# GroupNorm on one core: all stores issued from ScalarE's queue, and the last store in one piece

## Chip, core and metric

The kernel runs on one core of a Trainium2 chip. The metric is the device time of one execution in microseconds. A core has TensorE (PE), VectorE (DVE), ScalarE (ACT), GpSimd (POOL) and SyncE (SP). SP and ACT can issue transfers, which 16 DMA engines carry out.

## What is computed

A group normalisation of x, 128 x 1024 x 32 x 16 in bf16, with 32 groups of 32 channels:

```python
def reference(x, g, b):
    G = 32
    ...
    xr = x.reshape(B, G, C // G, H, W)
    mu = xr.mean(axis=(2, 3, 4), keepdims=True)
    var = ((xr - mu) ** 2).mean(axis=(2, 3, 4), keepdims=True)
    xn = (xr - mu) / jnp.sqrt(var + 1e-5)
    xn = xn.reshape(B, C, H, W)
    return xn * g[None, :, None, None] + b[None, :, None, None]
```

134 MB are read and 134 MB written.

## The kernel before

Two samples make a tile of 128 partitions x 8192 elements (2 MB): a partition holds 16 channels of one sample, and a pair of partitions is a group. There are 64 tiles, i = 0 to 63, in 11 buffers (`XBUFS`), normalised in place. Each tile goes through these steps, each a function of the code:

- L(i), line 121: SP issues the load.
- M1(i), line 137: ACT sums the last 2048 of the 8192 elements (from tile 2 on). M(i), line 154: PE sums the other 12 pieces of 512 over the partition pair, into PSUM.
- R(i), line 171: DVE reduces that to the negative mean.
- Q(i), line 189: ACT squares the tile less its mean and adds up, 7.12 us. Gm(i), line 206: PE sums over the pair.
- T(i), line 221: ACT takes the square root of the variance.
- A(i), lines 232 to 255: DVE makes the reciprocal, scale and bias, and normalises in 16 instructions.
- S(i), lines 264 to 274: SP issues the store. The last store, i = 63, is two transfers: partitions 0 to 119, then 120 to 127.

The loop runs these as a pipeline, s from -1 to 65. In iteration s the order in which instructions are recorded is M1(s+1), M(s+1), Gm(s-1), A(s-2), R(s+1), Q(s), T(s-1), S(s-2), L(s+7). Nine loads go out ahead of the loop (`PREFETCH`). `chain` fixes the order of each engine's instructions as they are recorded; so ACT's list repeats M1(s+1), Q(s), T(s-1), and SP's repeats S(s-2), L(s+7).

Waits are put in by the framework. Three kinds matter here. A load waits until the store that used its buffer has landed. An engine waits for data that another one makes: T(s-1) is recorded with a wait for R(s+1), which follows A(s-2) on DVE. And the transfers of both queues count their completions on eight semaphores, DMAHW0 to DMAHW7, handed out in rotation in the order of the program; a transfer is issued only when the previous one on its semaphore has landed, unless another wait implies that.

Of the kernel before, what the change touches and what calls it, by code (L numbers as in the profile page):

```python
# [24 lines left out]
def kernel(  # L25
# [7 lines left out]
    nc = tc.nc  # L33
    P = nc.NUM_PARTITIONS
# [5 lines left out]
    NT = B0 // NS  # L40
# [16 lines left out]
    o_v = out.rearrange("(t n) (cb k) h w -> t (n cb) (k h w)", n=NS, cb=CB)  # L57
# [19 lines left out]
    def chain(key, inst):  # L77
        prev = last.get(key)
        if prev is not None:
            tc.add_manual_dep(inst.ins, prev.ins.name, nosync, reason="pipeline order")  # L80
        last[key] = inst
        return inst
# [5 lines left out]
        out=ind_f[:].rearrange("p (a c) -> p a c", c=PPG),  # L88
        in_=ones_f[:].rearrange("p (a c) -> p a c", c=PPG),
# [7 lines left out]
        out=ind_f[:].rearrange("p (a c) -> p a c", c=PPG),  # L97
        in_=ind_f[:].rearrange("p (a c) -> p a c", c=PPG),
# [165 lines left out]

    def S(i):
        st = state[i]
        xt = st["xt"]
        if i == NT - 1:
            lo = P - P // 16
            chain("sp", nc.sync.dma_start(out=o_v[i][0:lo, :], in_=xt[0:lo, :]))  # L270
            chain("sp", nc.sync.dma_start(out=o_v[i][lo:P, :], in_=xt[lo:P, :]))
        else:
            chain("sp", nc.sync.dma_start(out=o_v[i], in_=xt[:]))
        state.pop(i - 3, None)

    for i in range(min(PREFETCH, NT)):
# [16 lines left out]
    for s in range(-1, NT + 2):  # L293
        if 0 <= s + 1 < NT:
            M1(s + 1)
            M(s + 1)
        if 0 <= s - 1 < NT:
            Gm(s - 1)
        if 0 <= s - 2 < NT:
            A(s - 2)  # L300
        if 0 <= s + 1 < NT:
            R(s + 1)
        if 0 <= s < NT:
            Q(s)
        if 0 <= s - 1 < NT:
            T(s - 1)
        if 0 <= s - 2 < NT:
            S(s - 2)
            if s - 2 + PREFETCH < NT:
                L(s - 2 + PREFETCH)  # L310
# [30 lines left out]
```

## Time and profile before

| | |
|---|---|
| median of 3 runs | 642.97 us (642.89 to 643.67) |
| the profiled execution's own time | 642.89 us |
| its span in the profile | 641.1 us |
| loads issued from SP | 64 of 2048 KB, 24.2 us to landing |
| stores issued from SP | 63 of 2048 KB, 28.7 us to landing; then 1920 KB and 128 KB |
| moved | 268.69 MB, mean 419 GB/s |
| Q on ACT, line 189 | x64, 7122 ns each |
| M1 on ACT, line 137 | x62, 1898 ns each |
| normalising on DVE, line 255 | x1024, 406 ns each |
| last store issued | 620.41 and 620.88 us from the span's start |

Busy time is summed over an engine's instructions and given as a share of the span. A "q" behind an engine's name is its sequencer, which reads the instructions, does the waits and issues transfers; those are not counted as busy. The time to landing runs from the issue to the last of a transfer's completions.

### The profile page before, as it was taken

Reading aid. Unit: us, or ns where it says so; the run is one execution under the profiler, and the core shown is the slowest. Engines: PE = TensorE matmul, PEld = TensorE weight load, DVE = VectorE, ACT = ScalarE, POOL = GpSimd, SP = SyncE. Lnnn points to the kernel's source line nnn. Section 1 sums busy time; section 2 is a strip of 40 time slices with the busy share of each in tenths; the row PEclk is TensorE's granted clock in tenths of the full one; section 3 lists DMA queues with packets and bytes.
Section 4 is the critical chain, followed back from the end, with each engine's and each line's share of the span. In section 5 each row is a group of like instructions: output and inputs, shape, how many; then the busy total and the mean of one; then the engine's idle time right before and its main releaser. Section 6 shows DMA issues by size and latency. Waiting matters only on the chain.

```text
span 641.1 us, 3917 instructions
## 1 busy us (share of the span) xinstructions
PE 333.1 (52%) x904; PEld 127.4 (20%) x904; DVE 420.7 (66%) x1349; ACT 590.6 (92%) x318; POOL 1.6 (0%) x6
## 2 busy tenths in 40 slices
PE   4655574556456545654664465466465454564200
PEld 1222121122112212221221122122121121222100
DVE  0076677668667766776686677667766866776760
ACT  0999999999999999999999999999999999999900
POOL 1000000000000000000000000000000000000000
PEclk9777767776776676667666766766666766767655
DMA  9999999999999999999999999999999999999993
GB/s 359 425 427 423 422 432 424 428 431 428 430 433 429 432 430 427 435 429 428 432 430 434 430 426 432 431 430 432 429 430 432 429 432 432 428 431 430 431 408 96
DMA packets 18781, 268.69 MB, mean 419 GB/s; under 512 B 2375, under 2 KB 2375, under 8 KB 2375
## 3 DMA queue, kind: packets, MB, share of 16 engines
q1 hardware_dynamic: 18759, 268.45, 98.6%
q8 instruction: 7, 0.11, 0.1%
q14 instruction: 15, 0.12, 0.0%
HBM read 134.23 MB, written 134.22 MB: 419 GB/s over the span
## 4 chain that ended last, share of the span: by engine, by line
ACT 56%; DMA 19%; issue 19%; DVE 2%; PE 1%; SPq 0%; DVEq 0%; ACTq 0%
ACT ja L189 41%; ACT ja L137 15%; DMA out_dram<-xt 14%; DMA xt<-in_x_dram 5%; DVE xt L255 2%; ACT rstd L221 1%; PE ps L154 1%; SPq L121 0%; DVE jd L171 0%; DVE scl L237 0%; DVE bia L243 0%; DVE rstd L232 0%; DVEq L336 0%; ACTq L137 0%
## 5 line engine op out<-in xcount | busy, mean ns | idle before, releaser
L189 ACT ACTIVATE ja<-xt,negmean 128x8192 bf16<-128x8192 bf16 x64 | 455.8, 7122 | 15.8 <-DVE jd L171 13.8
L154 PE MATMUL ps<-xt,ind_b 128*128 128x512 bf16 x776 | 307.7, 580 | 66.1 <-DMA xt<-in_x_dram 66.1
L255 DVE TENSOR_SCALAR xt<-xt,scl,bia 128x512 bf16<-128x512 bf16 x1024 | 336.3, 406 | 2.6 <-DVE bia L243 0.2
L154 PEld LDWEIGHTS <-ind_b 128*128 128x128 bf16 x776 | 109.1, 147 | 234.5 <-issue 164.3
L232 DVE RECIPROCAL rstd<-rstd 128x1 f32<-128x1 f32 x64 | 10.5, 163 | 168.7 <-ACT rstd L221 168.7
L137 ACT ACTIVATE ja<-xt 128x2048 bf16<-128x2048 bf16 x62 | 117.7, 1898 | 1.5 <-DMA xt<-in_x_dram 1.5
L243 DVE SCALAR_TENSOR_TENSOR bia<-scl,negmean,bet 128x16 f32<-128x16 f32 x64 | 15.0, 235 | 2.3
L237 DVE TENSOR_SCALAR scl<-gam,rstd 128x16 f32<-128x16 f32 x64 | 15.0, 234 | 2.2
L189 ACT ACTIVATION_READ_ACCUMULATOR ja<-xt,negmean 128x1 f32 x64 | 11.9, 186 | 0.0
L137 ACT ACTIVATION_READ_ACCUMULATOR ja<-xt 128x1 f32 x62 | 11.7, 189 | 0.0
L171 DVE TENSOR_SCALAR_CACHE_REDUCE jd<-ps 128x512 bf16<-128x512 f32 x2 | 1.4, 692 | 8.3 <-PE ps L154 8.3
L171 DVE TENSOR_SCALAR_CACHE_REDUCE jd<-ps,ps_170 128x512 bf16<-128x512 f32 x1 | 0.8, 756 | 6.6 <-PE ps_170 L206 6.6
L290 DVE CAST gam<-gam_b 128x16 f32<-128x16 bf16 x1 | 0.2, 175 | 6.6 <-DMA gam_b<-in_g_dram 6.6
L206 PE MATMUL ps_3186<-carry,ind_f 128*128 128x1 f32 x2 | 0.6, 364 | 6.7 <-ACT ja L189 6.7
L206 PE MATMUL ps_3157<-carry,ind_f 128*128 128x1 f32 x2 | 0.6, 363 | 4.9 <-ACT ja L189 4.9
L206 PE MATMUL ps_1959<-carry,ind_f 128*128 128x2 f32 x2 | 0.6, 365 | 4.8 <-ACT ja L137 4.8
L206 PE MATMUL ps_734<-carry,ind_f 128*128 128x2 f32 x2 | 0.6, 364 | 4.8 <-ACT ja L137 4.8
L206 PE MATMUL ps_1616<-carry,ind_f 128*128 128x2 f32 x2 | 0.6, 364 | 4.7 <-ACT ja L137 4.7
L206 PE MATMUL ps_391<-carry,ind_f 128*128 128x2 f32 x2 | 0.6, 364 | 4.7 <-ACT ja L137 4.7
L206 PE MATMUL ps_1273<-carry,ind_f 128*128 128x2 f32 x2 | 0.6, 364 | 4.6 <-ACT ja L137 4.6
L206 PE MATMUL ps_2155<-carry,ind_f 128*128 128x2 f32 x2 | 0.6, 365 | 4.6 <-ACT ja L137 4.6
L206 PE MATMUL ps_930<-carry,ind_f 128*128 128x2 f32 x2 | 0.6, 365 | 4.6 <-ACT ja L137 4.6
(319 smaller groups left out, 127.3 us busy)
## 6 DMA issues: line engine op xcount, KB each, us to landing
xt<-in_x_dram SPq DMA_DIRECT2D x64, 2048.0 KB, 24.2
out_dram<-xt SPq DMA_DIRECT2D x63, 2048.0 KB, 28.7
out_dram<-xt SPq DMA_DIRECT2D x1, 1920.0 KB, 18.9
out_dram<-xt SPq DMA_DIRECT2D x1, 128.0 KB
gam_b<-in_g_dram SPq DMA_DIRECT2D x2, 2.0 KB, 7.2
bet_b<-in_b_dram SPq DMA_DIRECT2D x2, 2.0 KB, 7.3
```

Source lines behind the costliest of these rows:

```text
L137: nc.scalar.activation(out=ja[:, 0 : na * MMN], in_=xt[:, (NMM - na) * MMN :], func=ACT.Identity, scale=-inv_n, accum_out=carry[:, 1:2],),
L154: nc.tensor.matmul(out=ps[:], lhsT=ind_b[:], rhs=xt[:, k * MMN : (k + 1) * MMN], start=(k == 0), stop=(k == npe - 1),),
L171: nc.vector.tensor_scalar(out=jd[:], in0=st["ps"][:], scalar1=-inv_n, scalar2=seed, op0=ALU.mult, op1=ALU.add, accum_out=negmean[:],),
L189: nc.scalar.activation(out=ja[:], in_=st["xt"][:], func=ACT.Square, bias=st["negmean"][:], scale=1.0, accum_out=carry[:, 0:1],),
L206: nc.tensor.matmul(out=ps2[:, 0:ncol], lhsT=ind_f[:], rhs=st["carry"][:, 0:ncol], start=True, stop=True,),
L221: nc.scalar.activation(out=rstd[:], in_=st["ps2"][:, 0:1], func=ACT.Sqrt, bias=eps_t[:], scale=inv_n),
L232: chain("dve", nc.vector.reciprocal(out=rstd[:], in_=rstd[:]))
L237: nc.vector.tensor_scalar(out=scl[:], in0=gam[:], scalar1=rstd[:], scalar2=None, op0=ALU.mult),
L243: nc.vector.scalar_tensor_tensor(out=bia[:], in0=scl[:], scalar=negmean[:], in1=bet[:], op0=ALU.mult, op1=ALU.add,),
L255: nc.vector.tensor_scalar(out=xt[:, k * HW : (k + 1) * HW], in0=xt[:, k * HW : (k + 1) * HW], scalar1=scl[:, k : k + 1], scalar2=bia[:, k ...
L290: nc.vector.tensor_copy(out=gam[:], in_=gam_b[:])
```

## The change

`S(i)` issues the store from ACT's queue and chains it into ACT's list, so that list repeats M1(s+1), Q(s), T(s-1), S(s-2). The last store is one transfer of 128 partitions, as the others are. SP's list holds only the loads and the four small ones of gamma and beta. Nothing else is edited; the semaphores of the transfers are handed out anew.

```diff
     def S(i):
         st = state[i]
-        xt = st["xt"]
-        if i == NT - 1:
-            lo = P - P // 16
-            chain("sp", nc.sync.dma_start(out=o_v[i][0:lo, :], in_=xt[0:lo, :]))
-            chain("sp", nc.sync.dma_start(out=o_v[i][lo:P, :], in_=xt[lo:P, :]))
-        else:
-            chain("sp", nc.sync.dma_start(out=o_v[i], in_=xt[:]))
+        chain("act", nc.scalar.dma_start(out=o_v[i], in_=st["xt"][:]))
         state.pop(i - 3, None)
```

The rows of the changed program that the prediction speaks of, with what each transfer waits for in place of the semaphore's number (the store's wait for A(i) is implied by T(i+1)):

```
ACT S7  (DMAHW5) waits S3 landed
ACT S8  (DMAHW7) waits S4 landed
...
ACT S53 (DMAHW1) waits S49 landed
ACT S54 (DMAHW2) waits L60 landed
ACT S55 (DMAHW3) waits S50 landed
ACT S56 (DMAHW4) waits L61 landed
ACT S57 (DMAHW5) waits S51 landed
ACT S58 (DMAHW6) waits L62 landed
ACT S59 (DMAHW7) waits S52 landed
SP  L60 (DMAHW2) waits L56 and S49 landed
```

## The prediction

> **What bounds the kernel now.** I read the page's busy shares first, then the stretches of the span, then the order of time around the end. S(i), L(i), M1(i), Q(i), T(i), A(i) and R(i) are the code's steps for tile i, counted from 0 to 63.
>
> ```profile
> PE 333.1 (52%) x904; PEld 127.4 (20%) x904; DVE 420.7 (66%) x1349; ACT 590.6 (92%) x318; POOL 1.6 (0%) x6
> ...
> DMA  9999999999999999999999999999999999999993
> ```
>
> Two things are full: ACT (92%) and the 16 DMA engines (9 in every slice but the last).
>
> ```profile
> 100.00:600.00 500.00, 276.58 (x743) 105.24 (x741) 352.14 (x1127) 496.82 (x266) 0.00 (x0) 0.68 1.01 430
> 600.00:620.00 20.00, 1.18 (x4) 1.01 (x4) 17.19 (x57) 8.72 (x7) 0.00 (x0) 0.50 1.00 429
> ...
> 624.00:630.00 6.00, 0.00 (x0) 0.00 (x0) 0.00 (x0) 0.00 (x0) 0.00 (x0) 0.50 0.81 235
> 630.00:640.00 10.00, 0.00 (x0) 0.00 (x0) 0.00 (x0) 0.00 (x0) 0.00 (x0) 0.50 0.12 43
> ```
>
> The last two columns are the DMA share and GB/s. From 100 to 620 us the transfers run at 430 GB/s without a pause. Then they fall off over 16 us: some engines are done, one still works. Each transfer counts 16 completions; those recorded in the trace spread ever wider: 1.1 us between first and last for L0, 9.9 us for the store that ended at 621.6. So one engine is latest and sets every "landed". Its pace is in SP's load issues, which wait for landings: 271.86 to 567.53 us over 30 tiles, 9.86 us a tile, or 4.93 us per transfer.
>
> ```profile
> 543.38 1.90 ACT L137 ACTIVATE ja<-xt 128x2048 bf16<-128x2048 bf16 x1
> ...
> 552.96 1.91 ACT L137 ACTIVATE ja<-xt 128x2048 bf16<-128x2048 bf16 x1 [0.20 <-DMA xt<-in_x_dram]
> ...
> 562.68 1.91 ACT L137 ACTIVATE ja<-xt 128x2048 bf16<-128x2048 bf16 x1 [0.32 <-DMA xt<-in_x_dram]
> ...
> 591.80 1.91 ACT L137 ACTIVATE ja<-xt 128x2048 bf16<-128x2048 bf16 x1 [0.32 <-DMA xt<-in_x_dram]
> ```
>
> These are M1(58), M1(59), M1(60) and M1(63). ACT's own pace is 9.29 us (301.92 to 311.21). Up to M1(58) it never waited for a load; from M1(59) it does, as the 9.86 us pace has eaten the nine tiles of lead. So ACT has almost no slack when the loads end, and the DMA tail (stores until 639.9 us, by the last completion) ends the span: last store issued at 620.4, a further 1.2 us from 639.9 to 641.1.
>
> **The change, part by part.**
>
> *64 stores leave SP.* SP's list then holds loads alone.
>
> ```profile
> SPq L121 <- DMA out_dram<-xt: 351.3, 48, 9.8
> SPq L273 <- DVE xt L255: 187.8, 29, 24.9
> ...
> SPq L273 <- DMA xt<-in_x_dram: 5.7, 2, 3.0
> ```
>
> A load waits for the store that frees its buffer (351.3 us in all). That wait stays: 11 buffers, so L(i) needs S(i-11) landed. Gone is only that L(i+9) stood behind S(i): L9 and L10 now go out early, at about 24 and 29 us, when L3 and L4 have landed. The DMA engines were full then anyway, so this gains nothing by itself; it puts two more loads ahead in the queue. [...]
>
> *64 issues come to ACT, each behind T(i+1).* One took SP 0.33 to 0.50 us.
>
> ```profile
> 303.94 7.12 ACT L189 ACTIVATE ja<-xt,negmean 128x8192 bf16<-128x8192 bf16 x1
> ...
> 308.64 0.09 DVE L171 DVE_READ_ACCUMULATOR jd<-ps,ps_1616 128x1 f32 x1
> ```
> ```profile
> L137 ACTq EVENT_SEMAPHORE  x1: 17/17/17, 308.8 to 308.8; - x1
> ```
>
> The second fence is the wait ahead of M1, which stands behind T in ACT's list. It ran at 308.77 us, right after VectorE's R (T's wait) and 2.3 us before Q ended at 311.07. So ACT's sequencer runs ahead of the engine: an issue of 0.46 us at 308.8 lies under Q. Cost 0; with that cover gone 0.42 us a tile. Data leave barely later: T's wait already implies A(i), so S0 goes at about 39.5 us, not 38.8.
>
> *Each store may now hold ACT.* This decides. Loads and stores share eight completion counters in rotation, and each transfer waits for the previous user of its counter. The changed program's waits read: S(i) waits S(i-4) for i from 7 to 53; then, since no loads are left to take turns, S54 waits **L60**, S56 L61, S58 L62. Before, the like waits stood on SP, where nothing followed but stores (the 5.7 us above). On ACT, M1(58) is behind S54, then Q(57), T(56) and all later tiles. But L60 is not needed for computing before M1(60). ACT is forced to be two tiles early with data that is just in time.
>
> When does L60 land? It is admitted when S49 has landed, and S53 is the last store out before S54. So when L60 lands, n = 50 to 54 stores have landed beside 61 loads; nothing else is possible. Before, L60 landed at 562.6 us (M1(60) above) with n = 52, as one queue serves S51 ahead of it. At 4.93 us each, it lands at 552.7 (n = 50) to 572.4 us (n = 54). Which n? At 41 us, when S0's data start, the queue holds 0.4 of L7 (landed at 43.1 before), L8, L9 and L10: 3.4 loads. From there each landed store admits one load; taking the alternation of before as the nearest row, one load lands per store and the backlog stays, less some 2 us of issue and first packet (0.2): 3.2. So L60 waits for 3.2 stores after S49: n = 53.2, landing at 562.6 + 1.2 x 4.93 = **568.5**. M1(58), which ran at 543.4, is 25 us late.
>
> From there ACT is the bound, with L61 to L63 and the counters of S55 to S63 free in time:
>
> - issue of S54 0.5, M1(58) to M1(63) 5 x 9.29 = 46.45
> - M1(63) to the last store's issue 620.4 - 591.8 = 28.6
> - that store, now alone: 8 rows per engine at 0.611 = 4.9 below, L0's 8.0 above; I take 7
> - last completion to end of span 1.2; span to time 642.89 - 641.1 = 1.8
>
> 568.5 + 0.5 + 46.45 + 28.6 + 7 + 1.2 + 1.8 = 654.0. The sum stands on the profiled execution, 642.89, 0.08 below the median of 642.97. The DMA engines then have 128 - 114.2 = 13.8 transfers left, 68 us of work in 82 us: they run dry.
>
> *The last store is whole again.* By the completions S61 ended at 626.4 on the latest engine, S62 8.0 us later instead of 4.9, and the two parts at 639.3 and 639.9. Packets that took 611 ns take 1200 to 2400 there: the 15-engine part disturbs what is still running. Whole: 626.4 + 2 x 4.9 = 636.2, 3.7 us less. It counts only if the DMA tail still ends the span; in the forecast it doesn't.
>
> **Rivals.**
>
> 1. *Loads get through first, ACT isn't held.* If fewer than 0.9 stores land between L60's admission and its landing (before 557.3 us), ACT ends early enough, and what remains is the mended tail: 636.2 + 1.2 + 1.8 = **639**. For it: loads would need precedence in each engine, and no row here shows two queues at once. Against: the backlog of 3.4 loads at 41 us. Between 556 and 559 it would end within 0.2%, 641.7 to 644.3, which is about what this measurement can tell from no change.
> 2. *Two queues cost rate.* The nearest row is the first stretch of mixed traffic, 42 to 66 us, at 421 GB/s against 430: 2.1%. Over the 527 us from 41 to 568 that is 11 us: **665**. Against: later mixed traffic runs at 430.
> 3. *The issue isn't hidden.* ACT's pace is 9.29 + 0.42 = 9.71. M1(58) would come at 543.4 + 55 x 0.42 = 566.5, so the wait for L60 hides it up to there; after that 5 tiles and 3 stores add 3.4: **657**. Against it is the wait that ran at 308.77.
>
> **Numbers.** Forecast 0.64; loads first 0.12 (0.08 faster, 0.04 same); rate 0.14; issue 0.10. Predicted 654. By n alone the forecast reaches from 638 to 658; n = 51 gives 643, below which I leave about 0.08, and the upper end 663 takes in issue and most of the rate case. Faster 0.08, same 0.04, slower 0.88.
>
> **What would show it.** One idle time of ACT of 15 to 25 us at about 545 to 568 us, ended by a load, ahead of an L137; 0 to 0.1 us around the other stores; the DMA share under 1 from about 590 us; the last store landing some 7 us after its issue; VectorE unchanged. If ACT has a gap at every T, it is rival 3; if GB/s from 100 to 500 is under 425, rival 2. I am wrong if L60 lands before 557 us, or if S54's wait passes without a gap.

## The result, and the profile after

| | before | changed |
|---|---|---|
| median | 643.29 us (642.89 to 643.67, 4 runs: the three above and one more) | 652.36 us (651.31 to 653.27, 4 runs) |
| profiled execution, its span | 642.89, 641.1 us | 651.92, 650.1 us |

The ratio is 1.0141, with a 95% interval from 1.0122 to 1.0159: 9.1 us slower. The forecast was 654 us.

First ACT's time around tile 58, from the changed kernel's timeline: start, duration, engine and line, and in brackets the idle time just before, with what ended it.

```profile
539.82 7.12 ACT L189 ACTIVATE ja<-xt,negmean 128x8192 bf16<-128x8192 bf16 x1
546.85 0.19 ACT L189 ACTIVATION_READ_ACCUMULATOR ja<-xt,negmean 128x1 f32 x1
546.94 0.24 ACT L221 ACTIVATE rstd<-ps_2841,eps_t 128x1 f32<-128x1 f32 x1
567.25 0.34 ACTq L267 DMA_DIRECT2D out_dram<-xt  x1
567.68 1.91 ACT L137 ACTIVATE ja<-xt 128x2048 bf16<-128x2048 bf16 x1 [20.50 <-DMA xt<-in_x_dram]
```

Q(56) and T(55) are done at 547.2. Then nothing, for 20.5 us. The store S54 is issued at 567.25, and M1(58) follows at 567.68. The idle time is put down to a load, but not to M1(58)'s own: by the trace's completions L58 had landed at 547.8. L60 landed at 567.22, 0.02 us ahead of the issue.

ACT's idle times (who waited for what: us in total, times, longest), from the changed kernel's table of waits:

```profile
ACT ja L137 <- DMA xt<-in_x_dram: 20.5, 1, 20.5
ACT ja L189 <- DVE jd L171: 13.2, 1, 13.2
ACT ja L137 <- ACT rstd L221: 2.1, 7, 0.3
ACT ja L137 <- DMA out_dram<-xt: 1.3, 1, 1.3
ACT L111 <- PEq L319: 0.8, 1, 0.8
ACT rstd L221 <- PE ps_3186 L206: 0.5, 1, 0.5
```

The 13.2 us are the start, which the kernel before has too (13.8). The one wait of 20.5 us is the loss; the first experiment takes it away. The 2.1 and 1.3 us are taken up below.

What the hold did to the transfers, in the changed kernel's stretches (the last two columns are the DMA share and GB/s):

```profile
100.00:500.00 400.00, 217.73 (x592) 83.51 (x591) 280.57 (x899) 396.43 (x214) 0.00 (x0) 0.68 1.01 430
500.00:560.00 60.00, 28.40 (x79) 11.20 (x77) 37.48 (x120) 45.79 (x25) 0.00 (x0) 0.67 1.01 431
560.00:600.00 40.00, 17.87 (x49) 7.14 (x50) 18.10 (x59) 32.19 (x18) 0.00 (x0) 0.63 0.95 405
600.00:620.00 20.00, 8.60 (x24) 3.11 (x22) 14.55 (x48) 19.94 (x11) 0.00 (x0) 0.67 0.52 220
620.00:630.00 10.00, 0.59 (x2) 0.50 (x2) 6.82 (x22) 10.00 (x4) 0.00 (x0) 0.50 0.50 210
630.00:640.00 10.00, 0.59 (x2) 0.50 (x2) 8.98 (x30) 1.03 (x4) 0.00 (x0) 0.50 0.74 315
```

Up to 560 us two queues move as much as one did: 430 GB/s. From 600 to 630 ACT is busy to the full and the transfers run at half rate, since tiles come at ACT's 9.29 us and only have to be stored. Before, 600 to 620 still had 429 GB/s. The bound at the end has passed from the DMA engines to ACT. M1(63) and the issue of the last store, which finds an empty queue, show its end:

```profile
614.13 1.90 ACT L137 ACTIVATE ja<-xt 128x2048 bf16<-128x2048 bf16 x1
...
642.73 0.34 ACTq L267 DMA_DIRECT2D out_dram<-xt  x1
```

And the issue itself, from the changed kernel's timeline:

```profile
303.34 7.12 ACT L189 ACTIVATE ja<-xt,negmean 128x8192 bf16<-128x8192 bf16 x1
...
308.15 0.34 ACTq L267 DMA_DIRECT2D out_dram<-xt  x1
...
310.61 1.90 ACT L137 ACTIVATE ja<-xt 128x2048 bf16<-128x2048 bf16 x1
```

ACT's sequencer issues for 0.34 us while the engine is inside Q. M1 to M1 is 9.29 us as before (301.32 to 310.61).

### The profile page after: what moved, and what is told of

The parts are those of the page before. It is cut to its first block, busy times and chain, and to the rows that moved or that the text cites. A ratio compares the mean times of both kernels' runs of the same rounds, so it can differ in the third digit from the quotient of the medians.

```text
span 650.1 us, 3950 instructions
## 1 busy us (share of the span) xinstructions
PE 329.1 (51%) x904; PEld 127.3 (20%) x904; DVE 420.8 (65%) x1349; ACT 591.1 (91%) x318; POOL 1.6 (0%) x6
## 2 busy tenths in 40 slices
DMA packets 18774, 268.69 MB, mean 413 GB/s; under 512 B 2368, under 2 KB 2368, under 8 KB 2368
## 4 chain that ended last, share of the span: by engine, by line
ACT 66%; issue 17%; DMA 12%; DVE 3%; PE 1%; ACTq 0%; DVEq 0%
ACT ja L189 48%; ACT ja L137 17%; DMA out_dram<-xt 6%; DMA xt<-in_x_dram 6%; DVE xt L255 2%; ACT rstd L221 1%; PE ps L154 1%; ACTq L267 0%; ACTq L137 0%; DVE bia L243 0%; DVE scl L237 0%; DVE jd L171 0%; DVE rstd L232 0%; DVEq L330 0%
## 5 line engine op out<-in xcount | busy, mean ns | idle before, releaser
L189 ACT ACTIVATE ja<-xt,negmean 128x8192 bf16<-128x8192 bf16 x64 | 455.8, 7122 | 15.2 <-DVE jd L171 13.2
L154 PE MATMUL ps<-xt,ind_b 128*128 128x512 bf16 x776 | 304.6, 575 | 85.9 <-DMA xt<-in_x_dram 85.9
L137 ACT ACTIVATE ja<-xt 128x2048 bf16<-128x2048 bf16 x62 | 117.7, 1899 | 24.0 <-DMA xt<-in_x_dram 20.5
```

Of the source, the lines that this page charges most:

```text
L137: nc.scalar.activation(out=ja[:, 0 : na * MMN], in_=xt[:, (NMM - na) * MMN :], func=ACT.Identity, scale=-inv_n, accum_out=carry[:, 1:2],),
L154: nc.tensor.matmul(out=ps[:], lhsT=ind_b[:], rhs=xt[:, k * MMN : (k + 1) * MMN], start=(k == 0), stop=(k == npe - 1),),
L189: nc.scalar.activation(out=ja[:], in_=st["xt"][:], func=ACT.Square, bias=st["negmean"][:], scale=1.0, accum_out=carry[:, 0:1],),
```

## Experiments

The theory: the whole loss is the hold of ACT by S54's wait for L60; the whole last store is worth 3 to 4 us, but only where the DMA tail ends the span. The rivals: two queues cost time as such; the split of the last store is neutral, or helps. "Before" was run beside them: 643.61 us in the first four, 643.63 in the last three.

### Dose: the hold taken away, and halved

`st_inst` keeps the store instructions. A dependence without a wait orders each load behind a store in the program, so that only the rotation of the eight semaphores, and with it what each transfer waits for, is another; each engine runs the same instructions in the same order:

```diff
-        chain("sp", nc.sync.dma_start(out=xt[:], in_=x_v[i]))
+        ld = chain("sp", nc.sync.dma_start(out=xt[:], in_=x_v[i]))
+        if i - PREFETCH in st_inst:
+            tc.add_manual_dep(
+                ld.ins, st_inst[i - PREFETCH].ins.name, nosync, reason="program order"
+            )
...
-        chain("act", nc.scalar.dma_start(out=o_v[i], in_=st["xt"][:]))
+        st_inst[i] = chain("act", nc.scalar.dma_start(out=o_v[i], in_=st["xt"][:]))
```

With `PREFETCH` 9, the store that waits for L60 becomes S56.

> Stores stay on ACT and the last store stays whole; a scheduling order without a wait puts L(i+9) behind S(i) in the program, so that the counters rotate otherwise: the store that waits for L60 is now S56, and M1(60), which stands next in ACT's list, needs L60 anyway. Theory (the hold of ACT by S54 is the whole loss): no idle time of ACT over 1 us after 100 us; M1(63) at about 596.5, when L63 has landed; last store issued at 625.1; the DMA tail ends it: eight stores of 4.9 us after 596.5, so 636.1 + 1.1 + 2 = 639. Rival (two queues cost time as such, the hold only shows where ACT happens to wait): 648 to 652.

Measured: 638.88 us (638.79 to 639.14), 0.9927 of before, interval 0.9914 to 0.9941. ACT's waits (M1 is line 142 here, R line 176):

```profile
ACT ja L194 <- DVE jd L176: 12.9, 1, 12.9
ACT ja L142 <- ACT rstd L226: 2.8, 9, 0.3
ACT ja L142 <- DMA out_dram<-xt: 2.6, 2, 1.3
ACT L111 <- PEq L324: 0.8, 1, 0.8
ACT ja L142 <- DMA xt<-in_x_dram: 0.7, 2, 0.3
```

The 20.5 us are gone, and with them 13.5 us of the time. M1(63) ran at 596.85, and the last completion is at 636.3 (expected 596.5 and 636.1):

```profile
596.85 1.91 ACT L142 ACTIVATE ja<-xt 128x2048 bf16<-128x2048 bf16 x1 [0.35 <-DMA xt<-in_x_dram]
```

The two stores that held ACT for 1.3 us each are more than the 1 us expected; they cost nothing at the end, since M1(63) waited for its own load.

With `PREFETCH` 10, S55 waits for L60, so ACT is held one tile early.

> As the run with the distance of 9, but L(i+10) behind S(i): the store that waits for L60 is S55, and M1(59) stands next. ACT is held one tile early instead of two. Theory: M1(59) at 567.7 as L60 lands at 567.2 again, one idle time of ACT of about 10 us ahead of it, M1(63) at 604.9, last store issued at 633.5, landed at 640, time 643, which is 9.3 us (one tile of ACT) less than the changed kernel's 652.4. Rival (the hold is not what sets the end): 652 or 639, the same as one of its neighbours.

Measured: 643.60 us (642.26 to 644.27), 0.9995 of before, 0.9987 to 1.0004. Its timeline:

```profile
567.46 0.34 ACTq L272 DMA_DIRECT2D out_dram<-xt  x1
567.90 1.91 ACT L142 ACTIVATE ja<-xt 128x2048 bf16<-128x2048 bf16 x1 [9.83 <-DMA xt<-in_x_dram]
```

This is M1(59), at the very time at which M1(58) ran in the changed kernel. Two tiles early 652.4, one 643.6, none 638.9. The first step is 8.8 us, nearly one tile of ACT. The second is smaller, 4.7, as without a hold the DMA tail ends the span. The theory stands, and the rival that two queues cost time as such falls: with the last store whole and no hold, two queues take 638.88 us, and one queue takes 639.46 (the next run).

### The last store alone, and the queue alone

The kernel before, with only the last store made whole:

```diff
-        if i == NT - 1:
-            lo = P - P // 16
-            chain("sp", nc.sync.dma_start(out=o_v[i][0:lo, :], in_=xt[0:lo, :]))
-            chain("sp", nc.sync.dma_start(out=o_v[i][lo:P, :], in_=xt[lo:P, :]))
-        else:
-            chain("sp", nc.sync.dma_start(out=o_v[i], in_=xt[:]))
+        chain("sp", nc.sync.dma_start(out=o_v[i], in_=xt[:]))
```

> The kernel before with the last store in one piece and nothing else changed. Theory (the part on 15 engines slows what is still running and the latest engine gets one row more): S62 and S63 each end 4.9 us after the one ahead on the latest engine, no packet over 700 ns after 620 us, last completion at 636.2 instead of 639.9, time 639.2. Rival 1 (the split is neutral): 643. Rival 2 (the split spares the latest engine, so whole is worse): 646 or more.

Measured: 639.46 us (639.04 to 640.0), 0.9936 of before, 0.9924 to 0.9949. Its stretches:

```profile
600.00:620.00 20.00, 1.18 (x4) 1.00 (x4) 17.09 (x56) 8.81 (x7) 0.00 (x0) 0.51 1.01 431
620.00:630.00 10.00, 0.00 (x0) 0.00 (x0) 0.49 (x2) 0.00 (x0) 0.00 (x0) 0.50 0.73 313
630.00:640.00 10.00, 0.00 (x0) 0.00 (x0) 0.00 (x0) 0.00 (x0) 0.00 (x0) 0.53 0.04 17
```

and the same ones of the kernel before:

```profile
620.00:630.00 10.00, 0.00 (x0) 0.00 (x0) 0.38 (x2) 0.00 (x0) 0.00 (x0) 0.50 0.91 297
630.00:640.00 10.00, 0.00 (x0) 0.00 (x0) 0.00 (x0) 0.00 (x0) 0.00 (x0) 0.50 0.12 43
```

Split, the engines are busier (0.91) and move less (297); whole, they are less busy (0.73) and move more (313). The same bytes took longer on the engines. After 615 us 61 data packets took over 700 ns in the kernel before, the longest 2485; with the whole store none. The last completion is at 636.2, as worked out.

The queue alone is the changed kernel with the split put back, both parts from ACT:

```diff
-        chain("act", nc.scalar.dma_start(out=o_v[i], in_=st["xt"][:]))
+        if i == NT - 1:
+            lo = P - P // 16
+            chain("act", nc.scalar.dma_start(out=o_v[i][0:lo, :], in_=xt[0:lo, :]))
+            chain("act", nc.scalar.dma_start(out=o_v[i][lo:P, :], in_=xt[lo:P, :]))
+        else:
+            chain("act", nc.scalar.dma_start(out=o_v[i], in_=xt[:]))
```

> The changed kernel with the last store in two parts again (partitions 0 to 119 and 120 to 127), both from ACT: the move of the queue alone. ACT is held by S54 as before, so 652.4 is the base. Theory 1 (the 120 partitions collide among themselves): the packets of the last store take 1200 ns or so even with nothing else under way, its landing takes 10 to 11 us instead of 6.3, time 656 to 657. Theory 2 (the part on 15 engines only disturbs what is still running, here nothing): 652.4 to 653, one row of 0.6 us at most.

Measured: 658.85 us (658.61 to 659.18), 1.0237 of before, 1.0223 to 1.0251: theory 1, and dearer than expected. From the DMA issues (size, then us to landing):

```profile
out_dram<-xt ACTq DMA_DIRECT2D x1, 1920.0 KB, 11.0
```

The first part's 11.0 us are as expected. The small part lands 1.8 us after it, at 655.9; theory 1 had no term for that. Nothing else was under way, and 104 of the 128 packets of this store took over 700 ns. The first 15, which had all started by 644.15, took 616 to 1280 ns, against a median of 611 in the kernel before. The small part was issued at 643.68, and the first part's own packets came 0.84 us after its issue, so these 15 are the first part's. The packets of the 120 partitions are thus slow with nothing else under way; how much the small part adds was not separated.

The move of the queue alone thus costs 15.2 us (658.85 - 643.61); the whole store gives 6.5 of it back (658.85 - 652.36). On the kernel before it gives 4.2 (643.61 - 639.46).

### What it is about the split

`lo = P // 2` in the kernel before: two halves of 64 partitions.

> The kernel before with the last store cut into partitions 0 to 63 and 64 to 127, both from SP: 16 engines each, four rows an engine. Theory (a store of fewer than 128 partitions gives the engines rows in another arrangement, in which they collide): many packets over 1000 ns after 620 us as with 120 and 8, last completion 2 us or more after that of the whole store (636.2), time 641.5 to 644. Rival (only the number of engines, 15 and 8, is at fault): 639.5 as with the whole store.

Measured: 642.95 us (641.76 to 643.61), 0.9991 of before, 0.9982 to 1.0. After 615 us 73 packets took over 1000 ns; the last completion is at 639.8. Both halves counted 16 completions: the packets under 512 B are 2384, 16 more than with the store whole (2368), against 7 more with 120 and 8 (2375). Taking one of these for one engine, which is my reading, all 16 engines worked on each half.

Two halves by columns, over all 128 partitions:

```diff
-            lo = P - P // 16
-            chain("sp", nc.sync.dma_start(out=o_v[i][0:lo, :], in_=xt[0:lo, :]))
-            chain("sp", nc.sync.dma_start(out=o_v[i][lo:P, :], in_=xt[lo:P, :]))
+            lo = F // 2
+            chain("sp", nc.sync.dma_start(out=o_v[i][:, 0:lo], in_=xt[:, 0:lo]))
+            chain("sp", nc.sync.dma_start(out=o_v[i][:, lo:F], in_=xt[:, lo:F]))
```

> The kernel before with the last store cut by columns, 4096 of 8192 elements each, so 128 partitions in both parts. Theory (the arrangement of partitions is at fault, not that there are two transfers): no packet over 700 ns after 620 us, time 639.5 as with the whole store, 0.3 more at most. Rival (a second transfer at the end costs in itself): 641 or more.

Measured: 639.37 us (638.7 to 639.5), 0.9934 of before, 0.9922 to 0.9947; no packet over 634 ns after 615 us. The first half went out 2.3 us earlier than the whole store, as it needs only half of A; that hides no cost, for the halves landed 2.4 us apart, at 634.1 and 636.5, half of the 4.9 us of a whole store. So it is not the second transfer nor, on that reading, the number of engines: a cut by partitions costs 3.5 us with halves and 4.2 with 120 and 8, a cut by columns nothing. Why the packets of a cut by partitions last longer, no run here shows.

### Why one DMA engine is latest

The kernel before with the store whole, and behind A eight memsets of one column:

```diff
+    def X(i):
+        for _ in range(8):
+            chain("dve", nc.vector.memset(pad[:], 0.0))
...
             A(s - 2)
+            X(s - 2)
```

> The kernel before with the last store whole, and eight VectorE memsets of 128x1 more for each tile, behind A: 512 instructions more, which VectorE has time for. It asks why one DMA engine is latest. Theory (it also brings VectorE's instructions; the steps of 0.8 us in SP's load issues come once per fetch, every 55 us): 512 x 64 B are four fetches of 8 KB more, the latest engine ends 4 x 0.78 = 3.1 us later, time 642.6. Rival (the lag has another cause): 639.5.

Measured: 643.26 us (642.57 to 644.52), 0.9994 of before, 0.9985 to 1.0003, so 3.8 us more than without the memsets. The instruction fetches of this kernel, and below of the one without memsets:

```profile
q14 instruction: 19, 0.16, 0.1%
```
```profile
q14 instruction: 15, 0.12, 0.0%
```

Four packets of 8 KB more for 512 instructions, 64 B for each, as expected, and the last completion at 640.5 instead of 636.2, 1.07 us for each; I had 0.78. The second-latest completion of that store moved by 2.1 us, as the loads and with them ACT's end came later too.

The times of the packets tie the lag to the fetches. Successive transfers land some 4.86 us apart, but in the kernel without memsets 10 of these intervals (from 60 us on) are 5.6 to 5.9 us, and with memsets 14 are 5.5 to 5.9: four more, as there are four more fetches. Each of the 24 long intervals holds one fetch of 8 KB from q14. Four fetches of each kernel, near 108, 236, 303 and 499 us, lengthen nothing. The ten steps sum to 8.8 us, most of the 10.3 us between the first and the last completion of S60. So the fetches that VectorE's instructions bring set the latest engine back. Which engine it is was not read from the trace, and why a packet of 0.31 us costs a step of 0.7 to 1.0 us stays open.

## Why the prediction was right

Point by point, with the profiled execution's own values:

| step | predicted | measured |
|---|---|---|
| n, in stores' worth of time, when L60 lands | 53.2 | 53.0 (S0 to S51 landed, and S52 0.2 us after L60) |
| L60 lands | 568.5 | 567.2 |
| S54 issued to M1(58) | 0.5 | 0.43 |
| M1(58) to M1(63) | 46.45 | 46.45 (614.13) |
| M1(63) to the last store's issue | 28.6 | 28.6 (642.73) |
| the lone last store | 7 (4.9 to 8.0) | 6.3 (649.0) |
| last completion to the end of the span | 1.2 | 1.1 |
| outside the span | 1.8 | 1.8 |
| sum | 654.0 | 651.9 |

The mechanism held, and so did the time. One load landed beside each store, as the prediction had taken it: L58 at 547.8 and S50 at 548.0, L59 at 557.5 and S51 at 557.7, L60 at 567.2 and S52 at 567.4. The 2.1 us too many are mainly two terms: the backlog of loads (3.2 taken, 3.0 met: 29.9 us from S49's landing at 537.3 to L60's, at 9.86 each), which is 1.3 us, and the landing of a store that meets an empty queue (0.7).

*Two queues at no cost* was taken without a row of before that has two queues; it held, with 430 GB/s from 100 to 500 us, and rival 2 falls. *The issue under Q* held: 0.34 us at 308.15, and M1 to M1 stayed 9.29, so rival 3 falls. *Loads first* (rival 1) fell on the backlog. Its price was right: without the hold, 638.9 against 639. *The whole store worth 3.7 us on the DMA tail and nothing in the forecast*: 4.2 on the kernel before. But "nothing" was wrong: with the split back in the changed kernel the time is 6.5 us longer. The prediction's reason, that the part on 15 engines disturbs what is still running, was too narrow: with no other transfer under way 104 of the 128 packets still took over 700 ns.

*"0 to 0.1 us around the other stores"* was wrong. S(i) waits for S(i-4), and that I took to be free. From M1(50) to M1(57) the spacing is 9.64 to 10.7 us instead of 9.29: the stores ahead of these wait, and hold ACT up to 1.3 us, for the landing of a store issued 40 us before. S53 went out at 537.31, just after S49 had landed at 537.3. That makes 4.3 us up to M1(57). The forecast was spared this error, since L60's landing set what came next. Where the hold is gone it is still there (the 2.8 and 2.6 us of the first experiment), and that kernel ends with the DMA tail.

Three versions beat both kernels: stores from ACT with the other rotation (638.9), the kernel before with the whole store (639.5), and with column halves (639.4). Their intervals overlap, so they are not told apart.

## What to carry to other kernels

When a transfer moves to an engine that computes, list everything its issue waits for: data, buffer and the semaphore's previous user. All that stands behind it in that engine's list inherits the wait: here M1(58) and what follows it, 20.5 us. Look above all at the end of the loop, where one of two kinds of transfers stops and a rotation that paired like with like begins to pair unlike ones; here an order in the program that adds no wait was worth 13.5 us. And where a store over all partitions has to be cut, try the free axis first: here that cost nothing (639.4 us against 639.5 whole), and the cut by partitions 3.5 to 4.2 us.

## What was not expected of the hardware

Two queues on the 16 DMA engines cost no rate here (430 GB/s with one and with both). A store cut by partitions moved at about half rate: 1920 KB took 11.0 us with only the other 128 KB under way, 2048 KB whole 6.3. And 32 KB of instructions were not free in this kernel, which the DMA tail ends: 512 tiny VectorE instructions, on an engine 66% busy, cost 3.8 us, with four more fetches of 8 KB and four more steps in the landings.
